# Top-k attention with a gated MLP on one core: the opening's steps issued in an order from a table

## The chip, the core and the metric

The kernel runs on one core of one Trainium2 chip. Five engines work beside each other, each through its own instructions in their order: TensorE (PE in the profile, PEld for its weight loads), VectorE (DVE), ScalarE (ACT), GpSimd (POOL) and SyncE (SP, which here only issues DMAs). Semaphores hold an instruction back until what it reads is written and what it overwrites is read. The metric is the device time in microseconds of one execution; lower is better.

## The reference

Two blocks behind each other. The first is attention over 8 batches and 8 heads, with 576 rows of 64 a head, in which each row keeps its 32 largest scores. The second is an MLP of width 2048 over the 4608 x 512 outputs, whose gate is h * sigmoid(1.702 h).

```python
scores = scale * np.matmul(q, k.transpose(0, 1, 3, 2))
kth = np.partition(scores, -top_k, axis=-1)[..., -top_k:-top_k + 1]
scores = np.where(scores >= kth, scores, -1000000000.0)
scores = scores - np.max(scores, axis=-1, keepdims=True)
attn = np.exp(scores)
attn = attn / (np.sum(attn, axis=-1, keepdims=True) + 1e-09)
x = np.matmul(attn, v)          # heads side by side: (4608, 512)
h = x @ w_in
return (h * (1.0 / (1.0 + np.exp(-1.702 * h)))) @ w_out
```

## The kernel before

**Slots.** The attention is cut into 144 slots, 18 a batch. A slot holds 128 query rows of two heads (of a pair `hp`), that is two score rows of 576 on each of 128 partitions; the last 64 rows of the heads are put together in slots of their own. A slot n goes through these steps, which are spread over later slots:

- `scores(n)` (L330, PE): eight matmuls into the one pair of score banks `s_ps`. `copy_scores(n)` (L345, ACT) copies them to `sc`, of which there are four buffers.
- `pair_up(n)` (L354, DVE): larger and smaller of each pair of columns, into `ranked`. It reads the bank for the last time, so `scores(n + 1)` waits for it.
- `topk(n)` (L374, DVE): four rounds of MAX8 (the eight largest, L386) and three of MATCH_REPLACE8 (remove them, L390) for each of the two halves. The first two rounds run over 288 columns ("half width"), the others over 576. `find` (L1063) issues these fourteen operations of a slot; behind the eighth it issues `pair_up` of the next slot, and behind the ninth `invert` of the slot before.
- `bounds(n)` (L399, POOL): threshold and maximum. `mask(n)` and `exps(n)` (L414, L422, ACT): two passes over each half, with the sum `den`.
- `invert(n)` (L433): 1e-9 is added to the two sums and the reciprocal `rden` is taken on DVE. Up to slot PAIRED = 11 the addition runs on DVE (L439), afterwards on POOL (L437).
- Up to slot 9: `divide` (L443, POOL) makes two diagonal matrices `by` from `rden`, and `turn` (L458) transposes and scales the weights by matmuls on PE, with copies to `pt` on ACT. From slot 10 on: `normalize` (L450, POOL), `split` (L486: a copy on ACT that puts high and low halves of the words apart, and a DMA `rows<-sc` to DRAM), and `turn_by_dma` (L494: a transposing DMA `pt<-rows`).
- `values` (L515), `values_at` (L548), `values_of_two` (L566): weights times v on PE, in two column halves j = 0, 1 of the array (weights of 128 x 64 elements); copies to `xT` on ACT.

**The MLP.** When the four head pairs of a block of 128 rows are there, it is taken in four units: `hidden` (L651, PE, x times w_in), `tanh` (ACT, with a copy `h`), `gate` and `combine` (L685, L702, POOL mostly), `project` (L755, PE, times w_out). The first two blocks ("whole") use matmuls with 128 x 128 weights, the later ones 128 x 64 weights, two of them side by side.

**The opening.** In slots 0 to 10 both weight matrices come in by 32 pieces, which `round_piece` (L136) rounds: `size` and `low` on ACT, `shift` on DVE (L158, TENSOR_SCALARs of 128 x 512), `put_sign` (L148), `add` (L151) and `pool_size` on POOL. `stay_warm` (L170) issues matmuls whose results nobody reads.

**What sets the order.** The order is the order of the calls. `opening()` (L907), then `slot(n)` (L949) for n = 0 to 10, `filling()` (L1138) with a list of steps for each of slots 11 to 20, and `steady_pair(n)` (L1175) for two slots at a time from 21 on. Each engine runs its instructions in the order in which they are issued. All DMAs of the part in question are on SP's queue but three. In `filling_slot` (L1099) a `load_v` that falls due is issued behind `find` and before `scores(n + 2)`; this happens in slot 20, for batch 1.

Of the kernel before, what the change touches and what calls it, by code (L numbers as in the profile page):

```python
# [9 lines left out]
ALU = mybir.AluOpType  # L10
ENG = mybir.EngineType
F32 = mybir.dt.float32
# [7 lines left out]
P = 128  # L20
# [9 lines left out]
TO_ZERO = 2.0**-100  # L30


@with_exitstack
def kernel(
    ctx: ExitStack,
# [23 lines left out]

    nc = tc.nc

    B, H, S, D = q.shape
    C = H * D
# [24 lines left out]
    STEADY = PAIRED + 2  # L90
# [5 lines left out]
    const = ctx.enter_context(tc.tile_pool(name="const", bufs=1))  # L96
# [19 lines left out]
    both_banks = [ps_p.tile([P, 512], F32, name=f"po{i}") for i in range(2)]  # L116

    ident = const.tile([P, P], F32, name="ident")
    make_identity(nc, ident[:])
    win = const.tile([P, CC, DFF], F32, name="win")  # L120
    wout = const.tile([P, FC, C], F32, name="wout")

# [47 lines left out]
    def stay_warm(count, of=ident[:]):  # L170

        none = both_banks[1][:]
        for i in range(count):
            nc.tensor.matmul(none[:, 0:P], lhsT=of, rhs=of, start=True, stop=True)

    def load(name, b, hp, queue=None):

        src = q if name == "q" else k
        if (b, hp) not in loaded:
            home, tag = (ptp, "pt") if b == 0 and hp % 2 else (prp, "pr") if b == 0 and hp else (loads, "qk_l")  # L180
            if b == 1 and hp % 2:
                parts = raws[:, 3, :].bitcast(F32), diagonals[:, 0, :]
                main, ends = [x.rearrange("p (t j d) -> p t j d", j=2, d=D) for x in parts]
                loaded[b, hp] = [main[:, 0:NF, :, :], ends, main[:, NF:, :, :]]
            else:
                t = home.tile([P, 2 * NF + 1, 2, D], F32, name="qk_l", tag=tag)
                loaded[b, hp] = [t[:, 0:NF, :, :], t[:, NF : NF + 1, :, :], t[:, NF + 1 :, :, :], t]
        t = loaded[b, hp]
        heads_of = (lambda j: of_load(name, t)[:, :, j, :]) if queue is None else (lambda j: heads_apart(name, t)[:, j, :, :])
        queue = queue or nc.sync  # L190
        if b > 0 or hp > 1:
            both = src[b, 2 * hp : 2 * hp + 2, 0:FULL, :].rearrange("j (p t) d -> p t j d", t=NF)
            queue.dma_start(of_load(name, t), both)
        else:
            for j in range(2):
                queue.dma_start(heads_of(j), src[b, 2 * hp + j, 0:FULL, :].rearrange("(p t) d -> p t d", t=NF))

        on = slice(0, TAIL) if name == "q" else slice(TAIL, P)
        queue.dma_start(t[1][on, 0, :, :], src[b, 2 * hp : 2 * hp + 2, FULL:S, :].rearrange("h p d -> p h d"))
# [44 lines left out]
    def prepare_ends(b, hp):  # L244
        ends = ps_t.tile([P, 512], F32, name="tp")[:, 0:P]
        turn_qk_ends(b, hp, ends)
        copy_qk_ends(b, hp, ends)
# [45 lines left out]
    def write_all():  # L293
        while writes:
            writes.pop(0)()
# [26 lines left out]
    N = len(slots)  # L322
    PER = N // B
    st = [{} for _ in slots]
# [108 lines left out]
    def invert(n):  # L433

        some = small.tile([P, 2], F32, name="some", tag="sums")
        if n > PAIRED:
            nc.gpsimd.tensor_scalar(some[:], st[n]["den"][:], 1e-9, None, op0=ALU.add)  # L437
        else:
            nc.vector.tensor_scalar_add(some[:], st[n]["den"][:], 1e-9)  # L439
        rden = st[n]["rden"] = small.tile([P, 2], F32, name="rden", tag="inverse")  # L440
        nc.vector.reciprocal(rden[:], some[:])  # L441

# [190 lines left out]
    class Block:  # L633
        def __init__(self, place, rows):
            self.place, self.rows = place, rows
            self.whole = len(blocks_seen) < WHOLE
            self.bank = 1 - len(blocks_seen) % 2
            blocks_seen.append(self)
            self.left = list(range(FC))
            if not self.whole:  # L640
                self.left = [h * (FC // 2) + 2 * u + c for u in range(4) for h in range(2) for c in range(2)]
            self.done = 0
# [202 lines left out]
    for n in by_slot:  # L845
        first = sum(map(len, list(by_slot.values())[:n]))
# [60 lines left out]
    def opening():  # L907

        stay_warm(8, v_tail[:, 0, :, :].rearrange("p j d -> p (j d)"))
        load("q", 0, 0, nc.sync)  # L910
        load("k", 0, 0, nc.scalar)
        for hp in range(2):
            for name in "qk":
                if hp:
                    load(name, 0, hp)
        for x in by_slot[0]:
            load_piece(x)
        prepare_first()
        scores(0)
        pair_first()  # L920
        stay_warm(2)
        for name in "qk":
            prepare_main(name, 0, 1)
        stay_warm(8)
        prepare_ends(0, 1)
        early.extend(round_piece(x) for x in by_slot[0])
        for piece in early:
            piece["size"]()
        scores(1)
        copy_scores(1)  # L930
        prepare_rest()
        for hp in range(2, NP):
            for name in "qk":
                load(name, 0, hp)
        load_v(0, 0)
        for x in by_slot[1]:
            load_piece(x)
# [161 lines left out]
    def filling_slot(n, beside, pool_ahead, behind, pool_behind, late=[]):  # L1099

        todo = later.pop(n, [])
        due = [(fn, args) for fn, args in todo if fn is prepare_by_dma]
        exponentials(n - 1)
        for fn in beside:
            fn()
        for fn in pool_ahead:
            fn()
        find(n, 8)
        for fn, args in todo:
            if fn is load_v:  # L1110
                fn(*args)
        scores(n + 2)
        if n == PAIRED:
            normalize(n - 1)
            split(n - 1)
            copy_scores(n + 2)
        else:
            copy_scores(n + 2)
            normalize(n - 1)
            split(n - 1)  # L1120
        write_all()
        for fn, args in todo:
            if fn not in (prepare_by_dma, load_v):
                fn(*args)
        turn_by_dma(n - 1)
        while turns:
            turns.pop(0)()
        for fn in pool_behind:
            fn()
        bounds(n)  # L1130
        for fn in behind + late:
            fn()
        for fn, args in due:
            fn(*args)
# [40 lines left out]
    def steady_pair(n):  # L1175

        begin, prepare_some = dues(n)
        if live(n - 1):
            exponentials(n - 1)
        combine()  # L1180
        merge_some(3)
        if n > STEADY + 8:
            project_one()
        if n == STEADY + 8:
            brought.pop(0)()
            leave_all()
# [24 lines left out]
        merge_some(3)  # L1211
        if live(n):
            mask(n)
            exps(n)
        tanh(True)
        tanh(True)
        prepare_some()
        project_one()
        find(n + 1, 8)
        if live(n + 3):  # L1220
            scores(n + 3)
        held = [m for m in (n - 3, n - 2) if live(m)]
        o = [ps_t.tile([P, 512], F32, name="o", tag="tp")[:, 0:P] for _ in held]
        values_of_two(held, o)
        if live(n):
            normalize(n)
            split(n)
        write_all()
        while turns:
            turns.pop(0)()  # L1230
        begin(1)
        if live(n):
            turn_by_dma(n)
        gate()
        if live(n + 3):
            copy_scores(n + 3)
        x_of_two(held, o)
        if live(n + 1):
            bounds(n + 1)

    def last_units():
# [7 lines left out]
        project_one()  # L1249
        leave_all()  # L1250

    with tc.manual_schedule():
        opening()
        for n in range(SETTLED + 1):
            slot(n)
        filling()
        for n in range(STEADY + 8, N + 2, 2):
            steady_pair(n)
        combine()
        while ready or to_gate or gated or to_combine or to_project:  # L1260
            last_units()
        merge_some(len(merging), nc.vector)
        write_all()
# [30 lines left out]
```

## Time and profile before

| | us |
|---|---|
| median of 3 runs | 1379.32 (1377.34 to 1382.84) |
| the profiled execution | 1379.59 |
| its span, first to last instruction | 1377.8 |
| PE busy | 1341.2 (97%) |
| DVE busy | 1286.0 (93%) |
| ACT busy | 1164.1 (84%) |
| POOL busy | 964.4 (70%) |
| mean granted clock of TensorE | 0.992 |

The profile is of one execution. Groups of instructions are given by line of the kernel, engine, operation and tiles, as `out<-in`, with their count. A matmul of 32-bit numbers leaves two records. The end of a matmul is modelled and reaches beyond the start of the next one, so durations on PE are read from start to start. Starts are counted from the span's beginning.

### The profile page before, as it was taken

What the parts mean: (1) busy time and instruction counts of PE and PEld (TensorE: products, weight loads), DVE (VectorE), ACT (ScalarE), POOL (GpSimd) and SP (SyncE); (2) the same over time, 40 slices, a digit from 0 to 9 for tenths busy, and PEclk for the clock granted to TensorE, in tenths of its full rate; (3) what the DMA queues carried; (4) which work ended last, traced back from release to release, by engine and by line L of the source; (5) the groups of instructions that cost most, each with busy time, mean ns of one, the idle gap of its engine ahead of it and who ended that gap; (6) DMA issues with size and microseconds to landing.
All of it is one profiled execution on the core that took longest, in us unless ns stands there. A gap on an engine that the chain in (4) does not pass through costs nothing.

```text
span 1377.8 us, 54398 instructions
## 1 busy us (share of the span) xinstructions
PE 1341.2 (97%) x22560; PEld 1205.0 (87%) x22560; DVE 1286.0 (93%) x3392; ACT 1164.1 (84%) x1930; POOL 964.4 (70%) x1758
## 2 busy tenths in 40 slices
PE   7789999999999999999999999999999999999998
PEld 5676578899999999999999999999998999999998
DVE  7999998999999999999999999999999999999912
ACT  6988887998889888988898988888888998888841
POOL 3776676777777776777777777677777777777770
PEclk8999999999999999999999999999999999999999
DMA  7551568787889786977898668988888768855640
GB/s 232 155 163 62 151 159 198 179 196 196 205 210 211 178 189 173 232 193 192 192 227 208 182 174 193 210 198 191 197 211 208 195 176 183 184 142 135 151 118 17
DMA packets 527223, 246.92 MB, mean 179 GB/s; under 512 B 458880, under 2 KB 505472, under 8 KB 526976
## 3 DMA queue, kind: packets, MB, share of 16 engines
q1 hardware_dynamic: 526544, 243.16, 71.5%
q8 instruction: 177, 2.90, 0.9%
q14 instruction: 70, 0.57, 0.1%
q10 hardware_dynamic: 432, 0.30, 0.1%
HBM read 46.01 MB, written 103.42 MB: 108 GB/s over the span
## 4 chain that ended last, share of the span: by engine, by line
PE 79%; DMA 3%; ACT 1%; issue 0%; POOL 0%; SPq 0%; DVE 0%; DVEq 0%; ACTq 0%; POOLq 0%
PE ph L662 32%; PE po L776 28%; PE o L586 10%; PE s_ps L339 9%; DMA pt<-rows 2%; DMA rows<-sc 1%; ACT pr L428 0%; ACT sc L418 0%; ACT sc L490 0%; ACT sc L350 0%; ACT halves L268 0%; ACT raws L794 0%; SPq L221 0%; POOL pr L454 0%; ACT h L681 0%
## 5 line engine op out<-in xcount | busy, mean ns | idle before, releaser
L386 DVE MAX8 top<-ranked 128x8 f32<-128x288 f32 (+1 forms) x1152 | 637.6, 596 | 0.0
L662 PE MATMUL ph<-xT,win 128*64 128x128 f32 (+1 forms) x8544 | 493.8, 273 | 0.0
L662 PEld LDWEIGHTS ph<-xT,win 128*64 128x64 f32 (+1 forms) x8544 | 469.4, 137 | 27.6 <-issue 24.1
L390 DVE MATCH_REPLACE8 ranked<-top,ranked 128x288 f32<-128x288 f32 (+1 forms) x864 | 462.4, 543 | 0.0
L490 ACT COPY sc<-pr 128x2304 uint16<-128x2304 uint16 x134 | 283.4, 2115 | 90.1 <-POOL pr L454 90.0
L454 POOL TENSOR_SCALAR pr<-pr,rden 128x576 f32<-128x576 f32 x268 | 197.9, 748 | 49.2 <-DVE rden L441 47.7
L428 ACT ACTIVATE pr<-sc,low 128x576 f32<-128x576 f32 x288 | 219.9, 769 | 0.0
L418 ACT ACTIVATE sc<-sc,cut 128x576 f32<-128x576 f32 x288 | 208.6, 779 | 4.7 <-POOL cut L404 4.7
L360 DVE TENSOR_TENSOR ranked<-s_ps,sc 128x576 f32<-128x576 f32 x286 | 201.8, 747 | 3.8 <-ACT sc L350 3.8
L776 PE MATMUL po<-raws,h 128*64 128x128 f32 x2112 | 205.3, 273 | 0.0
L776 PE MATMUL po<-wout,h 128*64 128x128 f32 x2112 | 205.3, 273 | 0.0
L350 ACT COPY sc<-s_ps 128x576 f32<-128x576 f32 x286 | 168.5, 642 | 26.9 <-PE s_ps L339 14.4
L437 POOL TENSOR_SCALAR some<-den 128x2 f32<-128x2 f32 x132 | 29.3, 222 | 221.6 <-ACT pr L428 221.4
L339 PE MATMUL s_ps<-qk_t 64*64 64x288 f32 x2304 | 177.6, 421 | 5.6 <-DVE ranked L360 4.4
L691 POOL TENSOR_TENSOR th<-th,h 128x512 f32<-128x512 f32 x134 | 171.8, 1282 | 11.2
L776 PE MATMUL po<-wout,th 128*64 128x128 f32 x2176 | 165.3, 273 | 0.0
L776 PEld LDWEIGHTS po<-raws,h 128*64 128x64 f32 x2112 | 133.8, 137 | 0.0
L776 PEld LDWEIGHTS po<-wout,h 128*64 128x64 f32 x2112 | 133.7, 137 | 0.0
L776 PEld LDWEIGHTS po<-wout,th 128*64 128x64 f32 x2176 | 127.8, 137 | 0.9 <-POOL wout L739 0.4
L339 PEld LDWEIGHTS s_ps<-qk_t 64*64 64x64 f32 x2304 | 76.2, 134 | 58.1 <-issue 14.8
L586 PE MATMUL o<-pt,v_l 128*64 128x128 f32 (+1 forms) x2240 | 124.8, 265 | 0.0
L586 PEld LDWEIGHTS o<-pt,v_l 128*64 128x64 f32 x2240 | 110.3, 137 | 10.1 <-issue 9.5
(118 smaller groups left out, 1647.5 us busy)
## 6 DMA issues: line engine op xcount, KB each, us to landing
rows<-sc SPq DMA_DIRECT2D x134, 576.0 KB, 4.0
qk_rows<-halves SPq DMA_DIRECT2D x24, 576.0 KB, 5.5
out_dram<-raws SPq DMA_DIRECT2D x68, 128.0 KB, 3.7
raws<-in_moe_w_in_dram SPq DMA_DIRECT2D x16, 512.0 KB, 5.1
raws<-in_moe_w_out_dram SPq DMA_DIRECT2D x16, 512.0 KB, 3.7
qk_l<-in_q_dram SPq DMA_DIRECT2D x28, 256.0 KB, 4.4
qk_l<-in_k_dram SPq DMA_DIRECT2D x28, 256.0 KB, 4.2
v_l<-in_v_dram SPq DMA_DIRECT2D x4, 1024.0 KB, 8.8
```

The lines of the kernel that those rows point to most:

```text
L339: nc.tensor.matmul(ps[rows, i, c, 0:HALF], lhsT=qT[b, hps[p]][on, cols], rhs=kT[b, hps[p]][on, FIRST[i] + c * HALF : FIRST[i] + (c + 1) * ...
L360: nc.vector.tensor_tensor(out=ranked[n][:, :, c, :], in0=a, in1=b, op=op)
L386: nc.vector.max(top[:, i, 8 * r : 8 * r + 8], of(r, i))
L390: nc.vector.match_replace(to, top[:, i, 8 * r : 8 * r + 8], of(r, i), LOWEST)
L418: nc.scalar.activation(sc[:, i, :], sc[:, i, :], AF.Prelu, bias=cut[:, i : i + 1], scale=SCALE, alpha=HUGE)
L428: nc.scalar.activation(pr[:, i * S : (i + 1) * S], sc[:, i, :], AF.Exp, bias=low[:, i : i + 1], accum_out=den[:, i : i + 1],)
L454: nc.gpsimd.tensor_scalar(pr[:, i, :], pr[:, i, :], st[n]["rden"][:, i : i + 1], 1.0, op0=ALU.mult, op1=ALU.mult)
L490: nc.scalar.copy(out=halves, in_=pr[:].bitcast(U16).rearrange("p (k h) -> p h k", h=2))
L586: nc.tensor.matmul(o[s][j * D : (j + 1) * D, cols], lhsT=lhsT, rhs=rhs, start=(s, j) not in halves[:k], stop=(s, j) not in halves[k + 1 :],)
L662: nc.tensor.matmul(ph[rows, i * P : (i + 1) * P], lhsT=win[:, c, f * P + rows.start : f * P + rows.stop], rhs=xs[:, x.place, c, :], start= ...
L691: nc.gpsimd.tensor_tensor(out=th[:], in0=th[:], in1=h, op=ALU.mult)
L776: nc.tensor.matmul(both_banks[bank][y * TAIL : (y + 1) * TAIL, to * P : (to + 1) * P], lhsT=a[:, i, :], rhs=weight(w, fs[i])[:, y, :], sta ...
```

## The change

Engine calls go through two small classes. While `nc.collected` is a list, a call is put into it and not issued. `opening`, the eleven `slot`s, `filling` and the `steady_pair`s of 21 and 23 are run so, and then `issue_in_order` issues the collected calls in the order of the table `ORDER` (a part "1600+2" stands for 1600 and 1601). Buffers are still handed out in the order of the code. From `steady_pair(25)` on everything is issued as before.

Besides, the addition of 1e-9 on DVE becomes a TENSOR_TENSOR with a tile `little` that is filled once, and `load_v` in `filling_slot` is no longer issued ahead of the scores but with the other due steps behind `split` and `write_all`.

```diff
+COLLECTED = 25
+
+ORDER = """
+8 11 0+8 9 12 10 13+2 38+4 15+2 24 22+2 25 17 33 26+5 18 31 34 32 19 35 42 36 43+3 20 37 46+4 21 97 50 56+4 98
...
+1526 1589 1476 1665 1510+2 1732+2 1481 1647 1662 1590+8 1527 1538 1555 1443 1528 1512+2 1667 1598+2 1734+2 1557
...
+1567 1477 1649 1568 1740+2 1575 1702+2 1559 1600+2 1641 1602+2 1571 1742+2 1569 1666 1744+2 1604+2 1669 1577
+1606+2 1572 1311 1670 1746+2 1608+6 1675 1533 1614+2 1748+2 1576 1534 1704+2 1671 1616+2 1750+2 1643 1618+2
+1771 1573 1620+2 1677 1622+2 1578 1642 1624+2 1444 1626+2 1636+4 1773 1644 1668 1770 1752+2 1656 1650 1754+2
+1653 1679 1628+2 1706+2 1645 1630+2 1672 1680+3 1654 1683 1772 1684 1673 1685+2 1659 1655 1674 1574 1687 1676
...
+"""
+
+
+class Engine:
...
+    def __getattr__(self, name):
+        do = getattr(self.engine, name)
+
+        def step(*args, **kwargs):
+            if self.engines.collected is None:
+                do(*args, **kwargs)
+            else:
+                self.engines.collected.append(lambda: do(*args, **kwargs))
+
+        return step
...
-    nc = tc.nc
+    nc = Engines(tc.nc)
...
+    little = const.tile([P, 2], F32, name="little")
+    nc.gpsimd.memset(little[:], 1e-9)
...
-            nc.vector.tensor_scalar_add(some[:], st[n]["den"][:], 1e-9)
+            nc.vector.tensor_tensor(out=some[:], in0=st[n]["den"][:], in1=little[:], op=ALU.add)
...
         find(n, 8)
-        for fn, args in todo:
-            if fn is load_v:
-                fn(*args)
         scores(n + 2)
...
         write_all()
         for fn, args in todo:
-            if fn not in (prepare_by_dma, load_v):
+            if fn is not prepare_by_dma:
                 fn(*args)
...
+    def issue_in_order():
+
+        steps, nc.collected = nc.collected, None
...
+        for i in order:
+            steps[i]()
+
     with tc.manual_schedule():
+        nc.collected = []
         opening()
         for n in range(SETTLED + 1):
             slot(n)
         filling()
-        for n in range(STEADY + 8, N + 2, 2):
+        for n in range(STEADY + 8, COLLECTED, 2):
+            steady_pair(n)
+        issue_in_order()
+        for n in range(COLLECTED, N + 2, 2):
             steady_pair(n)
```

In the part of the table that is shown, 1559 is the last MAX8 of slot 16 and 1674 its reciprocal. Of the numbers between them those on DVE are 1666, 1669, 1668 (find of slot 17, half width), 1675, 1677, 1679, 1672 (the same, full width), 1670, 1671 (pair_up of slot 18), and 1770 to 1773 (the first four operations of slot 18); before, 1662 to 1672 stood there.

More of the change, by code (lines that the diff above doesn't have):

```diff
@@ L30, with __init__ @@
 TO_ZERO = 2.0**-100
+COLLECTED = 25
+ORDER = """
[83 rows of a table added]
+"""
+class Engine:
+    def __init__(self, engines, engine):
+        self.engines, self.engine = engines, engine
+    def __getattr__(self, name):
[6 more added lines that the diff above has]
+        return step
+class Engines:
+    def __init__(self, nc):
+        self.collected = None
+        for name in ("tensor", "vector", "scalar", "gpsimd", "sync"):
+            setattr(self, name, Engine(self, getattr(nc, name)))
 @with_exitstack
@@ L118 @@
     ident = const.tile([P, P], F32, name="ident")
-    make_identity(nc, ident[:])
+    make_identity(tc.nc, ident[:])
+    little = const.tile([P, 2], F32, name="little")
+    nc.gpsimd.memset(little[:], 1e-9)
     win = const.tile([P, CC, DFF], F32, name="win")
@@ L1250, in last_units @@
         leave_all()
+    def issue_in_order():
+        steps, nc.collected = nc.collected, None
+        order = list(range(len(steps)))
+        if ORDER.split():
+            order = []
+            for part in ORDER.split():
+                first, _, count = part.partition("+")
+                order += range(int(first), int(first) + int(count or 1))
+        assert sorted(order) == list(range(len(steps)))
+        for i in order:
+            steps[i]()
     with tc.manual_schedule():
+        nc.collected = []
         opening()
```

77 rows, old and new, of the table ORDER are left out of this document.

## The prediction

> **What bounds the kernel now.** I read the page first, then the busy time by stage, then who waited for whom in the stretch that the change touches.
>
> ```profile
> span 1377.8 us, 54398 instructions
> PE 79%; DMA 3%; ACT 1%; issue 0%; POOL 0%; SPq 0%; DVE 0%; DVEq 0%; ACTq 0%; POOLq 0%
> ```
>
> The chain that ended last is PE's. The stages (columns: length, then busy time of PE, PEld, DVE, ACT, POOL, then PE's clock, DMA share, GB/s):
>
> ```profile
> 0.00:10.00 10.00, 8.96 (x77) 7.88 (x78) 1.91 (x7) 2.51 (x3) 1.12 (x9) 1.00 0.62 155
> 10.00:60.00 50.00, 36.37 (x292) 27.27 (x292) 48.99 (x126) 42.99 (x88) 31.34 (x39) 0.83 0.66 209
> 60.00:120.00 60.00, 52.98 (x518) 43.69 (x518) 58.06 (x147) 51.84 (x100) 42.25 (x51) 0.97 0.49 151
> 120.00:210.00 90.00, 84.42 (x880) 60.65 (x880) 85.45 (x230) 77.83 (x140) 65.09 (x92) 1.00 0.52 124
> 210.00:262.00 52.00, 49.89 (x944) 45.34 (x946) 47.92 (x125) 41.39 (x65) 35.88 (x66) 1.00 0.77 195
> 262.00:1200.00 938.00, 936.75 (x16772) 857.85 (x16768) 924.04 (x2446) 836.68 (x1351) 682.10 (x1304) 1.00 0.82 196
> 0.00:262.00 262.00, 232.62 (x2704) 184.82 (x2706) 242.34 (x631) 216.56 (x393) 175.69 (x256) 0.96 0.59 162
> ```
>
> The change collects the steps up to slot 24. In this execution the last of them on PE are the values of steady_pair(23):
>
> ```profile
> 261.15 1.97 PE L586 MATMUL o<-pt,v_l 128*64 128x128 f32 x32
> ```
>
> They end at 263.1. From 262 to 1200 PE idles 938 - 936.75 = 1.25 us. All that follows the collected steps is therefore a block of fixed length behind PE, and what PE gains before 263 us arrives at the end. DVE has 14 us of slack there, so it doesn't become the bound later. Before 262, PE idles 29.4 us and DVE 19.7, of which 8.1 in the first 10 us. DVE is the fuller one: it runs the searches, and PE's scores wait for the bank that it frees.
>
> What DVE and PE wait for (DVE from 10 us on, then PE from 10 us on; total us, times, longest):
>
> ```profile
> DVE some L439 <- ACT pr L428: 4.2, 8, 1.1
> DVE rden L441 <- POOL some L437: 3.7, 4, 1.2
> DVE ranked L360 <- ACT sc L350: 3.2, 2, 3.0
> ...
> PE tp L468 <- POOL by L448: 7.0, 4, 3.5
> PE tp L471 <- ACT pt L476: 6.0, 5, 3.2
> PE tp L237 <- ACT qk_t L234: 5.3, 2, 4.3
> PE s_ps L339 <- DVE ranked L360: 4.4, 5, 1.4
> ...
> PE o L586 <- ACT h L681: 1.4, 2, 0.8
> ```
>
> **The table: what it moves.** I numbered the steps in the order in which the code reaches them: 2,597, the last in steady_pair(23), which is just what the table holds. Against before, 430 of 480 steps stand at another place on DVE, 306 of 351 on ACT, 223 of 249 on POOL, 1,339 of 1,392 on PE, and on SP 4 of 125. Work is neither added nor removed by it, so each engine's floor is its busy time.
>
> *DVE's waits.* Two half-width operations and what followed them, and the groups of full width:
>
> ```profile
> 54.04 0.44 DVE L390 MATCH_REPLACE8 ranked<-top,ranked 128x288 f32<-128x288 f32 x1
> ...
> 54.47 0.44 DVE L390 MATCH_REPLACE8 ranked<-top,ranked 128x288 f32<-128x288 f32 x1
> 55.34 1.29 DVE L439 TENSOR_SCALAR some<-den 128x2 f32<-128x2 f32 x1 [0.43 <-ACT pr L428]
> L386 DVE MAX8 top<-ranked 128x8 f32<-128x576 f32 x100 | 72.4, 746 | 0.0
> L360 DVE TENSOR_TENSOR ranked<-s_ps,sc 128x576 f32<-128x576 f32 x50 | 35.3, 747 | 3.2 <-ACT sc L350 3.2
> ```
>
> invert(n) stands behind nine operations of find(n+1). Between slot 16's last MAX8 and its reciprocal (steps 1559 and 1674) there were eight half-width operations, two pair_ups and one MAX8 of full width; in the table seven of half width, two pair_ups and four of full width, among them slot 18's first four operations. By these rows (0.36 to 0.43 from start to start for half width, 72.4 / 100 or 35.3 / 50, about 0.7, for the others) this is 8 x 0.39 + 3 x 0.7 = 5.2 against 7 x 0.39 + 6 x 0.7 = 6.9 us. Counted so, from start to start, over slots 0 to 23, the mean is 4.4 before and 6.1 in the table.
>
> But ACT's side is stretched too: other steps are put between mask(n) and exps(n), and from mask's start to the end of exps the mean of ACT's own work grows from 2.7 to 3.5 us. Net 1.7 - 0.8 = 0.9 us a slot, against twelve waits for invert of 7.9 us, 0.66 each. Bounds 0 and 7.9; I take three quarters, 6, since the mean wait is less than what was put in front of it and the longest, 1.2, is more.
>
> *PE's cost.* The table mixes hidden, project and values one by one. I counted the changes of the weights' tile (128*128, 128*64, 64*64) between neighbouring steps: 83 before, 176 in the table, nearly all of the 93 more in slots 4 to 17, where hidden and project still use 128*128 and values 128*64. What one costs is seen where the same group has different neighbours:
>
> ```profile
> 61.35 1.09 PE L526 MATMUL o<-pt,v_l 128*64 128x128 f32 x16
> 62.28 0.39 PE L526 MATMUL o<-pt,v_e 128*64 128x128 f32 x4
> 62.49 1.04 PE L526 MATMUL o<-pt,v_l 128*64 128x128 f32 x16
> ...
> 73.87 1.09 PE L526 MATMUL o<-pt,v_l 128*64 128x128 f32 x16
> ...
> 75.11 3.84 PE L662 MATMUL po<-xT,win 128*128 128x128 f32 x32
> ```
>
> The same twenty matmuls take 62.49 - 61.35 = 1.14 us ahead of another 128*64 group and 75.11 - 73.87 = 1.24 ahead of a 128*128 one: 0.10 a change, 93 x 0.10 = 9.3 us. Besides, a 128*64 matmul alone: twenty in two halves take 1.14, 0.057 each, where the 32 of 128*128 take about 0.112 each (3.84 less its 0.27 tail). So two halves run beside each other, and one left without its partner costs between 0 and 0.055 a record more. By counting the unpaired ones in the table this is 0 to 7.3 us; I take 7.3, the row nearer to it.
>
> PE's floor is then 232.6 + 9.3 + 7.3 and 1.0 before its first matmul: 250.2 us. PE has to wait for something on top. In 210 to 262, already full, it idles 2.1 of 52 us, and 1.4 of these are behind h's copy on ACT, which the late rows of the next part push back, so 0.7 of 52; over 250 us that is 3.4. PE ends its collected steps at 253.6 instead of 263.1: **9.5 us earlier**.
>
> **v behind rows.** In slot 20 load_v's three DMAs go from before scores(22) to behind split(19)'s rows. First SP's queue, with the microseconds that each issue took, then who waited, then from issue to landing for rows(19), for v, and for rows as a median:
>
> ```profile
> 223.72 2.82 SPq L282 DMA_TRANSPOSE qk_t<-qk_rows  x1
> 226.58 0.59 SPq L210 DMA_DIRECT2D v_l<-in_v_dram  x1
> 227.22 1.49 SPq L221 DMA_DIRECT2D v_e<-in_v_dram  x2
> 228.76 1.14 SPq L492 DMA_DIRECT2D rows<-sc  x1
> ...
> 237.00 1.18 ACT L350 COPY sc<-s_ps 128x576 f32<-128x576 f32 x2 [4.63 <-DMA rows<-sc]
> ...
> 238.22 1.42 DVE L360 TENSOR_TENSOR ranked<-s_ps,sc 128x576 f32<-128x576 f32 x2 [2.99 <-ACT sc L350]
> ...
> 228.76 8.15 DMA rows<-sc
> ...
> DMA to landing us min/median/max: 6.8/6.8/6.8
> ...
> rows<-sc SPq DMA_DIRECT2D x134, 576.0 KB, 4.0
> ```
>
> rows(19) goes out at 226.6 instead of 228.8, and not behind v's megabyte (8.15 us to landing, the median is 4.0). With the median it lands by 231 instead of 236.9; copy_scores(23) loses its 4.6 us of wait and DVE 3.0. Behind v on SP stands turn_by_dma(19), which waits for rows anyway. v goes out 1.1 us later and is first needed by values of slots 18 and 19 at 243; it had landed 6.8 us after 226.6, so some 8 us of cover stay.
>
> **1e-9 as a tile.** A TENSOR_TENSOR takes the place of twelve TENSOR_SCALARs on DVE.
>
> ```profile
> L439 DVE TENSOR_SCALAR some<-den 128x2 f32<-128x2 f32 x12 | 7.0, 582 | 4.2 <-ACT pr L428 4.2
> L441 DVE RECIPROCAL rden<-some 128x2 f32<-128x2 f32 x24 | 3.8, 160 | 4.1 <-POOL some L437 3.7
> 55.27 1.34 POOL L148 TENSOR_SCALAR raws<-raws 128x512 f16<-128x512 f32 x1
> ```
>
> At 55.34 the addition of two numbers takes 1.29 us, and ends at 56.63 when POOL's put_sign ends at 56.61: it waits out POOL's instruction. A small operation alone is 0.15 to 0.17. The trace has no addition of two SBUF tiles beside a busy POOL: if it is free, 7.0 - 12 x 0.15 = 5.2 us go; if it waits likewise, what counts is where it stands, and in the table 5 of the 12 have a POOL instruction unfinished by the sum of durations before them (2.9 us of rest), so 7.0 - 1.8 - 2.9 = 2.3 go. I take 2.3, the row being that of the operation it replaces. SBUF — State Buffer of the Trainium skill, Who interferes with whom, speaks against this edit: a VectorE instruction with two SBUF inputs contends with a GpSimd one that reads SBUF. No run here shows it yet; by it the 2.3 stands, without it 5.2.
>
> **The sum.** DVE: 262.0 - 6 - 3.0 - 2.3 = 250.7 us, 11.3 earlier. PE: 9.5 earlier. The later one decides: 9.5. This execution took 1379.59 us (1377.8 and 1.8 around it), 0.27 above the median. 1379.6 - 9.5 - 0.3 = **1370 us**.
>
> **Rivals.** *Better than that*: if halves need no partner, PE ends at 246.3 and DVE decides; with all 11.1 us of its waits and 5.2 of the additions gone, 16.3: **1363**. For it, every wait was given more room; against it, ACT's stretch. Chance 0.1.
>
> *The waits only change their place* (no change): DVE's waits come from ACT, which has 216.6 us of work in 262 and runs in order; if its longer stretch from mask to exps eats the room, only the 2.3 and load_v's 3.0 stay, and PE's extra 16.6, which the 29.4 idle cover, take back some: **1376 to 1382**. Against it: 0.9 us net a slot. Chance 0.21. If the additions are blocked everywhere, it costs 2.3 of the forecast: 1372.
>
> *Slower*: PE's tile changes become the path. PE runs in order, and a score that stands behind unpaired halves starts late; DVE then waits for it instead of for ACT. From scores(9) on (94 us before) PE's counted work is 8.8 us more than before. If its idle time there (5.6 in 120 to 210, 2.1 after it) stays, and nothing is gained ahead of it, the end moves by 8.8: **1388**. It decides when PE reaches scores(13) later than DVE has freed the bank; by the sums of work these are level there (about 129 us each). For it: the table's mixing; against it: 20.6 us of PE idle in 10 to 120. Chance 0.17.
>
> **How the numbers follow.** Forecast 0.52, with its own range 1366 to 1374 (PE's waits twice 3.4, or DVE's 11.3). A measurement can tell about 0.5% (6.9 us, here 1372.4 and 1386.2) from no change. Faster: 0.1 + nine tenths of 0.52, and 0.03 of the third case, 0.6; slower 0.17; within 0.23. Range 1363 to 1384, which leaves the slower case out.
>
> **What would show it.** DVE's waits L439 and L441 together fall from 7.9 to about 2; pair_up has no wait of 3 us; PE's idle before 250 falls from 29 to 14 or less while its busy time there rises by 10 to 17; additions take 0.15 to 1.3 us as POOL runs; and the first search of slot 25 starts near 251. The forecast is wrong if PE's busy time in the collected part doesn't rise, or if its end there stays at 260 or later.

## The result, and the profile after

The changed kernel takes **1388.4 us**, the median of six runs (1386.9 to 1394.5), against 1377.5 for the kernel before in the same comparison (six runs, 1374.7 to 1382.8). The ratio is 1.0084 with an interval of 1.0065 to 1.0103: slower by 11 us, where 9.5 us less were forecast. The profiled execution took 1388.0 us, with a span of 1386.2.

The page of after, its span, the busy time of the engines and the chain that ended last. All steps that the table issues carry one line, L133, and those issued directly behind them L131:

```profile
span 1386.2 us, 54405 instructions
...
PE 1358.3 (98%) x22560; PEld 1208.6 (87%) x22560; DVE 1277.7 (92%) x3392; ACT 1164.2 (84%) x1930; POOL 963.2 (69%) x1759
...
PE 89%; ACT 3%; DVE 2%; DMA 2%; issue 1%; POOL 0%; DVEq 0%; ACTq 0%; SPq 0%
PE ph L131 31%; PE po L131 27%; PE o L131 9%; PE s_ps L131 9%; PE po L133 6%; PE o L133 2%; PE tp L133 2%; PE s_ps L133 2%; PE ph L133 1%; DMA pt<-rows 1%; DMA rows<-sc 1%; ACT sc L133 1%; DVE ranked L133 1%; ACT sc L131 1%; DVE top L131 1%
```

The chain now runs through PE's collected steps (po, o, tp, s_ps and ph of L133, 13% of the span together). The work is the same, as many PE records, and yet PE is busy for 1358.3 us where it was 1341.2: 17.1 more. Its idle time, the span less the busy time, fell from 36.6 to 27.9, 8.7 less. The span's 8.4 us are the difference of these two. Where each of them lies is in the stages of after, with the columns as before:

```profile
0.00:10.00 10.00, 8.54 (x62) 7.33 (x62) 0.94 (x5) 1.87 (x2) 1.15 (x10) 1.00 0.67 152
10.00:60.00 50.00, 35.36 (x284) 25.63 (x281) 44.99 (x125) 39.75 (x81) 30.85 (x36) 0.90 0.69 211
60.00:120.00 60.00, 59.05 (x462) 41.59 (x461) 47.49 (x123) 46.00 (x90) 34.98 (x44) 1.00 0.40 124
120.00:210.00 90.00, 89.36 (x840) 61.61 (x837) 83.86 (x229) 76.99 (x140) 65.03 (x86) 1.00 0.47 122
210.00:262.00 52.00, 50.41 (x954) 46.05 (x950) 50.13 (x132) 46.21 (x74) 37.30 (x69) 1.00 0.84 193
262.00:1200.00 938.00, 935.37 (x16718) 856.26 (x16716) 921.79 (x2443) 834.94 (x1348) 679.91 (x1302) 1.00 0.81 196
0.00:262.00 262.00, 242.71 (x2582) 182.22 (x2584) 227.42 (x611) 210.82 (x384) 169.32 (x244) 0.98 0.58 155
```

From 60 to 210 us PE is busy for 148.4 of 150 us, and does it with fewer records than before (1,302 against 1,398): the same matmuls take longer. DVE, which was busy for 58.1 of the 60 us from 60 to 120, is at 47.5. The bound has gone from DVE to PE. Before 60 us PE idles 16.1 us (14.7 before); from 60 to 262 it idles 3.2 (14.7 before).

The last collected work on PE, in its timeline, is a projection of eight records; it ends at 269.9 where the collected part ended at 263.1 before:

```profile
267.53 1.97 PE L133 MATMUL o<-pt,v_l 128*64 128x128 f32 x32
269.33 0.61 PE L133 MATMUL po<-wout,h 128*64 128x128 f32 x8
269.77 0.61 PE L131 MATMUL po<-wout,th 128*64 128x128 f32 x8
```

So 6.8 us of the loss stand at the end of the collected part. The account closes: 17.1 more work, 11.5 less idle time from 60 to 262 and 1.4 more ahead of it make 7.0; the rest of the 8.4 is idle time behind 262.

These busy times are not all at one speed. The clock column has 0.83 and 0.97 in the stages from 10 to 120 us before, and 0.90 and 1.00 in after: there are stretches in which the granted clock is 0.50, and a group takes nearly twice as long in them. In the kernel before, sixteen records of values that take 62.28 - 61.35 = 0.93 us in the rows of the prediction have taken 51.47 - 49.71 = 1.76 one slot earlier, in such a stretch (its row of the stage view first):

```profile
49.70:52.04 2.34, 2.34 (x24) 2.00 (x20) 2.34 (x5) 1.61 (x2) 0.62 (x2) 0.50 0.81 249
49.71 1.97 PE L526 MATMUL o<-pt,v_l 128*64 128x128 f32 x16
51.47 0.64 PE L526 MATMUL o<-pt,v_e 128*64 128x128 f32 x4
```

In the collected part these stretches are 18.2 to 21.7, 25.1 to 31.9, 45.5 to 52.4 and 103.6 to 107.0 us before, and 31.2 to 38.0 and 51.6 to 55.1 us in after; PE is busy for 18.1 and for 7.2 us in them. By these rows 0.47 of that time is lost to the clock, so after is 10.9 x 0.47 = 5.1 us better off (an estimate), and at one clock the table's added work is some 22 us rather than 17.1. What decides where these stretches lie was not tested.

What the added work is can be read in PE's timeline, where the table alternates hidden units, turns and values one matmul at a time (a matmul of whole width leaves two records here):

```profile
81.14 0.43 PE L133 MATMUL tp<-by,pr 128*64 128x128 f32 x2
81.50 0.49 PE L133 MATMUL po<-xT,win 128*128 128x128 f32 x2
81.92 0.43 PE L133 MATMUL o<-pt,v_l 128*64 128x128 f32 x2
82.28 0.49 PE L133 MATMUL po<-xT,win 128*128 128x128 f32 x2
82.70 0.43 PE L133 MATMUL o<-pt,v_l 128*64 128x128 f32 x2
83.06 0.49 PE L133 MATMUL po<-xT,win 128*128 128x128 f32 x2
```

One whole matmul of hidden and one half of values take 82.28 - 81.50 = 0.78 us. In streams of one shape, by the rows of the prediction, they take two records of 0.112 and two of 0.057, 0.34. The 0.44 more are two changes of shape and a half without a partner.

DVE's waits from 10 to 270 us in after (total, times, longest):

```profile
DVE th L133 <- ACT th L133: 10.6, 6, 3.1
DVE ranked L133 <- ACT sc L133: 5.6, 4, 2.6
DVE win L133 <- POOL win L133: 4.2, 1, 4.2
DVE some L133 <- ACT pr L133: 3.4, 5, 1.3
DVE rden L133 <- POOL some L133: 1.8, 1, 1.8
```

The waits that the table was counted on to remove, some and rden, fell from 7.9 to 5.2. A new one of 10.6 stands above them: gate waits for a tanh, and tanh for a hidden unit (ACT's own wait for it grows from 7.7 to 8.9 us).

### The profile page after: what moved, and what is told of

It reads as the page before. It is cut to its first block, busy times and chain, and to the rows that moved or that the text cites. A ratio compares the mean times of both kernels' runs of the same rounds, so it can differ in the third digit from the quotient of the medians.

```text
span 1386.2 us, 54405 instructions
## 1 busy us (share of the span) xinstructions
PE 1358.3 (98%) x22560; PEld 1208.6 (87%) x22560; DVE 1277.7 (92%) x3392; ACT 1164.2 (84%) x1930; POOL 963.2 (69%) x1759
## 4 chain that ended last, share of the span: by engine, by line
PE 89%; ACT 3%; DVE 2%; DMA 2%; issue 1%; POOL 0%; DVEq 0%; ACTq 0%; SPq 0%
PE ph L131 31%; PE po L131 27%; PE o L131 9%; PE s_ps L131 9%; PE po L133 6%; PE o L133 2%; PE tp L133 2%; PE s_ps L133 2%; PE ph L133 1%; DMA pt<-rows 1%; DMA rows<-sc 1%; ACT sc L133 1%; DVE ranked L133 1%; ACT sc L131 1%; DVE top L131 1%
## 5 line engine op out<-in xcount | busy, mean ns | idle before, releaser
L131 DVE MAX8 top<-ranked 128x8 f32<-128x288 f32 (+1 forms) x952 | 526.4, 595 | 0.0
L131 PE MATMUL ph<-xT,win 128*64 128x128 f32 x8064 | 464.3, 273 | 0.0
L131 PEld LDWEIGHTS ph<-xT,win 128*64 128x64 f32 x8064 | 441.2, 137 | 25.9 <-issue 22.8
L131 DVE MATCH_REPLACE8 ranked<-top,ranked 128x288 f32<-128x288 f32 x714 | 381.8, 542 | 0.0
L131 ACT COPY sc<-pr 128x2304 uint16<-128x2304 uint16 x120 | 253.8, 2115 | 88.5 <-POOL pr L131 88.5
L131 POOL TENSOR_SCALAR pr<-pr,rden 128x576 f32<-128x576 f32 x240 | 176.7, 747 | 42.5 <-DVE rden L131 42.5
L131 PE MATMUL po<-wout,h 128*64 128x128 f32 x2000 | 194.3, 273 | 0.0
L131 PE MATMUL po<-raws,h 128*64 128x128 f32 x2000 | 194.3, 273 | 0.0
L131 ACT ACTIVATE pr<-sc,low 128x576 f32<-128x576 f32 x240 | 183.4, 771 | 0.5 <-DMA qk_rows<-halves 0.5
L131 ACT ACTIVATE sc<-sc,cut 128x576 f32<-128x576 f32 x240 | 174.3, 782 | 0.1
L131 DVE TENSOR_TENSOR ranked<-s_ps,sc 128x576 f32<-128x576 f32 x236 | 166.6, 747 | 1.7 <-ACT sc L131 1.7
L131 POOL TENSOR_SCALAR some<-den 128x2 f32<-128x2 f32 x120 | 26.5, 220 | 203.5 <-ACT pr L131 203.5
L131 POOL TENSOR_TENSOR th<-th,h 128x512 f32<-128x512 f32 x123 | 157.3, 1279 | 10.3
L131 PE MATMUL po<-wout,th 128*64 128x128 f32 x2064 | 156.6, 273 | 0.0
L131 ACT COPY sc<-s_ps 128x576 f32<-128x576 f32 x234 | 137.9, 642 | 15.9 <-PE s_ps L131 9.4
L131 PE MATMUL s_ps<-qk_t 64*64 64x288 f32 x1872 | 140.5, 415 | 0.6 <-DVE ranked L131 0.6
L131 PEld LDWEIGHTS po<-raws,h 128*64 128x64 f32 x2000 | 126.4, 137 | 0.0
L131 PEld LDWEIGHTS po<-wout,h 128*64 128x64 f32 x2000 | 126.4, 137 | 0.0
L131 PEld LDWEIGHTS po<-wout,th 128*64 128x64 f32 x2064 | 121.2, 137 | 0.0
L131 PE MATMUL o<-pt,v_l 128*64 128x128 f32 (+1 forms) x2144 | 120.8, 267 | 0.0
L131 PEld LDWEIGHTS o<-pt,v_l 128*64 128x64 f32 x2144 | 106.6, 137 | 9.8 <-issue 9.4
L131 POOL TENSOR_TENSOR h<-th 128x128 f32<-128x128 f32 x248 | 113.7, 458 | 0.3
```

The source lines that it names most:

```text
L131: do(*args, **kwargs)
```

## Experiments

Two theories. **A**: PE pays for the order; changes of the weights' tile make its work longer in slots 4 to 17, where it has no idle time to take that from. **B**: the opening loses; the table lets queues wait for pieces of the weights ahead of the first slots' work. The kernel before had 1376.9 to 1377.3 us beside these runs. Step 411 is the first of slot 4.

**Without the table.** The other two edits alone: `ORDER = ""`.

> The table is empty: the collected steps are issued in the order of the code. What stays is the addition of 1e-9 as a tile and v behind rows. Theory A (PE's tile changes and unpaired halves, counted at 16.6 us, are the whole loss) and theory B (the loss comes from the opening, where ACT waits for weight pieces ahead of the scores' copies) both put the loss into the table: at or below the time before, 1370 to 1377 us. Theory C (one of the two small edits costs the time): 1383 or more. In the profile the additions take about 0.16 us if POOL doesn't hold them, 0.5 if it does, and copy_scores(23) doesn't wait 4.6 us for rows.

Measured: 1376.66 us, ratio 0.9996 (0.9983 to 1.0009). The loss is the table's. From 10 to 270 us DVE's waits are, in this kernel:

```profile
DVE rden L49 <- POOL some L49: 4.9, 4, 2.3
DVE some L49 <- ACT pr L49: 4.6, 8, 1.3
...
DVE ranked L49 <- ACT sc L49: 0.2, 1, 0.2
```

pair_up's 3.0 us of wait behind v's loads are gone, as forecast, and nothing of it shows in the time. The stage from 210 to 262 us of the same kernel has PE busy for 50.4 of 52 us, so an earlier DVE has nothing to hand it:

```profile
210.00:262.00 52.00, 50.40 (x958) 46.07 (x960) 49.71 (x133) 43.58 (x70) 37.44 (x70) 1.00 0.81 195
```

**PE's calls in one piece.** The table, but all matmuls of one call into one tile stand together, at the place of the last of them:

```
+        order = whole(order, nc.calls)
...
+def whole(order, calls):
+    last = {calls[i]: i for i in order if calls[i]}
...
+        elif last[calls[i]] == i:
+            out += [j for j in range(len(calls)) if calls[j] == calls[i]]
```

> The table stays on DVE, ACT, POOL and SP; on PE the matmuls of one call into one tile stand together, where the last of them stood. Tile changes on PE fall from 176 to about 92, unpaired halves to none. Theory A: PE's busy time in the collected part falls by about 16 us, to 234, and the time by 9 to 16, to 1372 to 1379 us. Theory B: scores(3) is still some 7 us late and DVE carries this to the end: 1383 to 1388, though PE's busy time falls as well.

Measured: 1391.23 us, ratio 1.0093 (1.0069 to 1.0118); above the ranges of both theories. PE's work fell, as theory A says, from 1358.3 to 1346.6 us over the span, but its idle time rose from 27.9 to 43.9. PE's waits from 10 to 262 us in this kernel:

```profile
PE s_ps L148 <- DVE ranked L148: 12.5, 5, 7.6
PE tp L148 <- POOL by L148: 5.6, 5, 2.4
PE tp L148 <- ACT xT L148: 3.5, 2, 3.0
```

The longest of them, 7.6 us, is not new (7.5 in after); the others are spread over many steps. That a whole group at its last member's place holds up what stands behind it is a reading that these rows don't prove. The edit changed two things, so it doesn't decide between A and B.

**Each part of the table alone.** First steps 0 to 410 in the code's order and the rest by the table, then the other way round:

```
+        order = list(range(411)) + [i for i in order if i >= 411]
+        order = [i for i in order if i < 411] + list(range(411, len(steps)))
```

> Steps 0 to 410 (the opening and slots 0 to 3) in the order of the code, the others in the table's order. By counting, 161 tile changes and 5.7 of the 7.3 us of unpaired halves stay, so 13 of the 16.6 us. Theory A: PE is still busy without a gap from 60 us on, 1383 to 1388 us. Theory B: ACT's waits for weight pieces and the late scores(3) are gone, 1374 to 1380.

> The reverse: steps 0 to 410 in the table's order, the others in the order of the code. By counting, 96 tile changes, and 2.6 us of the 16.6 stay. Theory A: 1374 to 1380 us. Theory B: ACT waits 6 us for weight pieces before 30 us, scores(3) is late by 6 to 8, and what DVE has lost isn't made good: 1382 to 1388.

Measured: 1389.50 us, 1.0079 (1.0056 to 1.0102), and 1382.70, 1.0036 (1.0026 to 1.0046). The first is 1.5 us above theory A's range, the second is in theory B's: neither theory has the whole of it. The table behind the opening makes the whole loss by itself, and in two stages of code_then_table PE is as full as in after, 147.9 of 150 us:

```profile
60.00:120.00 60.00, 58.37 (x463) 40.74 (x464) 50.05 (x133) 45.19 (x87) 34.52 (x45) 1.00 0.40 127
120.00:210.00 90.00, 89.56 (x856) 62.08 (x852) 84.49 (x228) 77.75 (x137) 67.00 (x90) 1.00 0.49 126
```

The opening's order alone costs 5.7. They don't add up. One reading is that DVE's lateness from the opening is hidden once PE is the bound; another part is the clock, for PE is busy for 16.0 us at the clock of 0.50 in code_then_table and for 7.2 in after. ACT's timeline in table_then_code shows what the opening's order does:

```profile
23.33 0.68 ACT L133 ACTIVATE win<-raws 128x512 f32<-128x512 f32 x1 [3.36 <-DMA raws<-in_moe_w_in_dram]
27.37 1.22 ACT L133 ACTIVATE raws<-raws 128x512 int32<-128x512 uint32 x2 [3.36 <-DMA raws<-in_moe_w_in_dram]
...
30.78 1.47 ACT L133 ACTIVATE sc<-sc,cut 128x576 f32<-128x576 f32 x2
```

ACT waits twice for pieces of w_in, and slot 0's mask behind them starts at 30.8 instead of 20.4 us.

**Halves.** A test of A that leaves the table's order and its numbering as they are: in the collected part each whole matmul of hidden, project and turn becomes two of 64 weight columns inside its step, so that it has the shape of the values.

```
+    def halves(self, out, lhsT, rhs, **kwargs):
...
+        def step():
+            for y in rows:
+                self.engine.matmul(out[y, :], lhsT=lhsT[:, y], rhs=rhs, **kwargs)
...
-                nc.tensor.matmul(tp[:, c * P : (c + 1) * P], lhsT=pr[:, at : at + P], rhs=by)
+                nc.tensor.halves(tp[:, c * P : (c + 1) * P], lhsT=pr[:, at : at + P], rhs=by)
```

> Kernel after, except that in the collected part each 128x128 matmul of a row block's hidden units, of its projection and of a slot's main turn is issued as two 128x64 halves inside one step, so that these no longer differ in shape from the values and the table's numbering stays. Same table. Counted in the table: tile changes 176 -> 98 (83 in the code's order), and a single values half no longer stands between two matmuls of another shape. Theory 'PE pays for the order' (the loss is tile changes and unpaired halves after 60 us, where PE has no idle time to give): PE's busy time in 60 to 210 falls from 148.4 us to 134 to 142 us, and the time from 1388.4 to 1375 to 1382 us; not further, since the opening stays as late as it is. Rival 'the opening' (scores late by waits for pieces of weights): 1386 to 1390 us. Rival 'shapes cost nothing, something else stretches PE': PE's busy time in 60 to 210 stays above 146 us and the time at 1388 us.

> The same edit (128x128 matmuls of the collected part as two 128x64 halves) without the table, steps in the code's order: a control. Tile changes 83 -> 73, so 1 us of PE at most: every theory expects 1374 to 1378 us. If it is faster than that, the halves help by themselves, and after_halves is to be held against it.

> Steps 0 to 410 (opening and slots 0 to 3) in the code's order, the rest by the table, with 128x128 matmuls of the collected part as two halves. Tile changes 161 -> 88. Theory 'PE pays for the order': 1389.5 - 73 x 0.10 - up to 5.7 for unpaired halves = 1376.5 to 1382 us; if the table's removal of waits on DVE is worth anything, this is the kernel that shows it, 1372 to 1376 us. Rival 'the opening': no different from code_then_table, 1389 us.

Measured: 1377.23 us, ratio 1.0000 (0.9990 to 1.0010); 1374.63, 0.9982 (0.9969 to 0.9994); 1375.80, 0.9989 (0.9976 to 1.0002). With the same table, the change of shape alone takes the time from 1388.4 back to 1377.2. Held against the same shapes in the code's order, the table still costs 2.6 us (1377.2 against 1374.6), where it cost 11.7 with whole matmuls (1388.4 against no_table's 1376.7). PE's busy time from 60 to 210 us is 144.9 us, above the 134 to 142 that theory A expected, and below the 146 of the theory that shapes cost nothing. The page of after_halves, the engines:

```profile
PE 1343.3 (98%) x23040; PEld 1202.4 (87%) x23040; DVE 1278.0 (93%) x3392; ACT 1164.6 (85%) x1930; POOL 965.8 (70%) x1759
```

15.0 us of PE's work are gone. In its timeline the same mixture as above now runs at 0.05 us a record:

```profile
81.16 0.27 PE L144 MATMUL po<-xT,win 128*64 128x128 f32 x1
81.22 0.27 PE L133 MATMUL tp<-by,pr 128*64 128x128 f32 x1
81.27 0.27 PE L133 MATMUL o<-pt,v_l 128*64 128x128 f32 x1
81.33 0.27 PE L144 MATMUL po<-xT,win 128*64 128x128 f32 x1
81.38 0.27 PE L133 MATMUL o<-pt,v_l 128*64 128x128 f32 x1
```

Without the table the halves leave 1338.1 of PE's work:

```profile
PE 1338.1 (97%) x23040; PEld 1199.9 (87%) x23040; DVE 1282.7 (93%) x3392; ACT 1164.6 (85%) x1930; POOL 962.7 (70%) x1759
```

What the table does to PE is thus 1358.3 - 1342.3 (no_table) = 16.0 us with whole matmuls, and 1343.3 - 1338.1 = 5.2 with halves.

**The price of one change.** No table; in the row blocks behind the second, every other unit of a hidden group uses whole matmuls where all used halves, which is the same work with three or four changes of shape more in each of 136 groups (four were expected; where scores follow a group, the last change was there before).

```
-                parts = 1 if x.whole else 2
+                parts = 1 if x.whole or i % 2 else 2
```

> Code order (no table), and in every row block after the second the odd ones of the four units of a group use one 128x128 matmul where they used two 128x64 halves: the same work, with 4 changes of tile shape in each of the 136 groups, 544 more than before, nearly all in the part where PE is always busy. It prices a tile change by itself. Theory 'PE pays for the order', at 0.10 us for a change: 1377 + 54 = 1425 to 1437 us. Rival 'a change costs nothing': 1377 us.

Measured: 1463.71 us, 1.0625 (1.0609 to 1.0641). That is above what theory A expected. Neighbouring records of different shape number 800 in its trace and 323 in that of the kernel before: 477 more, and not the 544 of the expectation. 86.4 us for 477 changes are **0.18 us each**, not 0.10. A group of hidden, from its start to that of the scores behind it, takes 4.18 us in mixed_tiles (its label names the first shape alone; the x48 are 32 records of halves and 16 of whole matmuls):

```profile
705.38 4.24 PE L47 MATMUL ph<-xT,win 128*64 128x128 f32 x48
709.56 0.47 PE L47 MATMUL s_ps<-qk_t 64*64 64x288 f32 x4
```

and 3.60 us in the kernel before:

```profile
707.61 3.66 PE L662 MATMUL ph<-xT,win 128*64 128x128 f32 x64
711.21 1.19 PE L339 MATMUL s_ps<-qk_t 64*64 64x288 f32 x15
```

That is 0.58 us for the three changes that are new here, 0.19 each.

**What is left.** For the opening, table_then_code with 17 steps on pieces of the weights moved behind slot 0's exponentials; for PE, after_halves and code_then_halves with the remaining transposes as halves and the two halves of a block side by side, and the same transposes without the table:

```
+        late = [164, 185, 215, 186, 183, 214, 187, 195, 261, 277, 213, 259, 165, 256, 193, 291, 260]
+        order = [i for i in order if i not in late]
+        order[order.index(161) + 1 : order.index(161) + 1] = late
...
+        order = paired(order, nc.pairs)
...
+def paired(order, pairs):
...
+    last = {pairs[i]: i for i in order if pairs.get(i)}
...
+        elif last[key] == i:
+            out += sorted(j for j in order if pairs.get(j) == key)
```

> Kernel table_then_code (opening and slots 0 to 3 by the table, the rest in the code's order), with 17 steps on pieces of the weights (four loads on SP, seven size and low steps on ACT, two shifts on DVE, four steps on POOL) moved, in the table's own order among themselves, from between the first and the last of slot 0's masks and exponentials to behind them. In table_then_code those steps wait for transfers of pieces until 23.3 and 27.4 us, and slot 0's cut comes at 28.0 instead of 20.1 us and its first mask at 30.8 instead of 20.4 us. Theory 'the opening loses by queues that wait for pieces': the mask comes back to 20 to 24 us and the time falls from 1382.7 to 1376.5 to 1379.5 us. Rival 'the opening loses by the order of its searches on DVE', which this leaves alone: 1381 to 1384 us.

> Kernel after_halves (whole table), and besides: the 16 transposes of later q and k columns that the table moves are issued as two halves too, and the two halves of one block of values, of a turn's ends or of a hidden unit, where the table sets them apart, stand together at the place of the later one. Tile changes 98 -> some 80, and no half without its partner. Theory 'PE pays for the order': at 0.16 us for a change and for the unpaired halves together 3 to 6 us off after_halves's 1377.2: 1371 to 1375 us. Rival 'what is left is waits, not PE's work' (values at the later place hold up the scores behind them, as in pe_whole): 1376.5 to 1380 us.

> The same as after_pairs, with steps 0 to 410 in the code's order: the table where it takes waits off DVE, with neither its tile changes nor its opening. Theory 'PE pays for the order': 1375.8 - 3 to 5 = 1371 to 1373.5 us, the fastest of all, and faster than no_table_pairs. Rival: 1375 to 1378 us.

> Control: no table, 128x128 matmuls of the collected part and those transposes as two halves. 7 tile changes less than no_table_halves: 1373.5 to 1375 us by either theory. What code_then_pairs gains over this one is what the table is worth by itself.

Measured: 1383.97 us, 1.0050 (1.0035 to 1.0065); 1378.45, 1.0011 (0.9997 to 1.0026); 1376.93, 0.9998 (0.9989 to 1.0008); 1376.65, 0.9994 (0.9984 to 1.0003). None reached what the first theory expected of it; the first three lie where the rivals had them, and the control 1.7 us above its range. In pieces_behind slot 0's mask does come back:

```profile
23.36 1.44 ACT L133 ACTIVATE sc<-sc,cut 128x576 f32<-128x576 f32 x2 [0.80 <-POOL cut L133]
```

but the time doesn't. Cuts of slots 0 and 1 start at 23.1 and 35.4 us, against 20.1 and 30.3 in the kernel before and 28.0 and 37.3 in table_then_code: the wait was moved more than taken away, for ACT now waits 2.73 us for a piece at 31.9, ahead of slot 1's mask. What the opening loses by stays open. In after_pairs PE's work is 1344.4 us, no less than in after_halves: between neighbours of its own shape a half without a partner costs nothing that shows in single executions.

All kernels side by side, from the first lines of their pages (idle is the span less PE's busy time):

| kernel | median us | span | PE busy | PE idle |
|---|---|---|---|---|
| before | 1377.5 | 1377.8 | 1341.2 | 36.6 |
| after | 1388.4 | 1386.2 | 1358.3 | 27.9 |
| no_table | 1376.7 | 1379.5 | 1342.3 | 37.2 |
| pe_whole | 1391.2 | 1390.5 | 1346.6 | 43.9 |
| code_then_table | 1389.5 | 1389.0 | 1359.4 | 29.6 |
| table_then_code | 1382.7 | 1382.4 | 1345.5 | 36.9 |
| after_halves | 1377.2 | 1374.4 | 1343.3 | 31.1 |
| no_table_halves | 1374.6 | 1372.9 | 1338.1 | 34.8 |
| code_then_halves | 1375.8 | 1373.7 | 1342.9 | 30.8 |
| mixed_tiles | 1463.7 | 1462.5 | 1429.5 | 33.0 |
| pieces_behind | 1384.0 | 1380.2 | 1344.7 | 35.5 |
| after_pairs | 1378.5 | 1375.5 | 1344.4 | 31.1 |
| code_then_pairs | 1376.9 | 1374.1 | 1340.8 | 33.3 |
| no_table_pairs | 1376.7 | 1375.7 | 1342.7 | 33.0 |

These are single executions, and the clock is in them: PE is busy at the clock of 0.50 for 14.4 us in no_table_halves and for 20.8 in no_table_pairs, which by the rate above is 3.0 of the 4.6 us between their busy times. Against no_table_halves, the table takes 3.7 us of PE's idle time (34.8 to 31.1; 4.0 in code_then_halves) and adds 5.2 (4.8) to its work, with 25 (15) changes of shape more. Against no_table_pairs, after_pairs has 1.9 us less idle time and 1.7 more work, and code_then_pairs 0.3 more and 1.9 less. So no gain from the table is shown: whatever waits it takes out, the time of no kernel with it is below that of the same shapes without it. no_table_halves is the one kernel whose interval lies below 1, by 0.2%, and no_table_pairs, with a little more of the same, doesn't confirm it.

## Why the prediction was wrong

*The step that failed* is the line "PE's floor is then 232.6 + 9.3 + 7.3 and 1.0 before its first matmul: 250.2 us" with the 3.4 us that PE would wait on top. It put the added work and the idle time of the whole collected part into one sum, as if the one could fill the other wherever it stands. The added work lies in slots 4 to 17, from 60 us on. Of the 29.4 us of idle time, 14.7 lie ahead of 60 us, where PE has nothing it could do yet, and they stay (16.1 in after). From 60 us on there were 14.7 to take, and PE took 11.5 of them. Forecast were 4.4 us of idle time in the collected part; 19.3 were left before 262. That difference, 14.9, is the way from the forecast end of 253.6 to 268.5; it was 269.9. The stage table of before held both numbers, and the sum went by its last row.

*PE's added work* came out right as a sum, 17.1 us where 16.6 were forecast, but that is partly luck: its terms were wrong, and the clock is in none of them. A change costs 0.18 instead of 0.10, since the row that gave 0.10 showed only the first start of the new shape, and the next one is late too: in mixed_tiles's trace a whole record starts 0.20 us behind the last half and the second one 0.21 behind the first, where 0.10 and 0.11 are usual. 93 x 0.18 = 16.7 stand where the sum had 9.3. Of the some 22 us at one clock this leaves about 5.5 for the halves without partners, by what remains, where 7.3 were taken; the 5.1 us that the clock gave back (an estimate, above) bring the sum down to 17.1.

*DVE's waits*, 6 of 7.9 us taken as saved: 5.2 were left of 7.9 in after, and 4.1 (1.3 and 2.8) in after_halves, 2.7 and 3.8 of the 6 (in no_table they are 9.5, so the table itself takes out 4.3). The cuts of slot 24, which end DVE's collected searches, show what it is worth. In after_halves, in no_table_halves and in code_then_halves, the last collected one starts at:

```profile
L133 POOL TENSOR_SCALAR cut<-top x1: 227/227/227, 256.9 to 256.9; 128x4 f32<-128x4 f32 x1
```

```profile
L49 POOL TENSOR_SCALAR cut<-top x1: 228/228/228, 257.1 to 257.1; 128x4 f32<-128x4 f32 x1
```

```profile
L133 POOL TENSOR_SCALAR cut<-top x1: 227/227/227, 256.4 to 256.4; 128x4 f32<-128x4 f32 x1
```

0.2 and 0.7 us are between the table and the code's order, and the same cut starts at 259.3 in no_table_pairs, so that is inside the spread. Whether an order that keeps the table's places on DVE and PE's groups in one piece would do better wasn't tried in a form that leaves the scores where they are.

*The opening* isn't in the prediction at all. It followed the waits for invert from slot to slot, and not ACT's queue ahead of slot 0's mask, where rounding steps now wait for transfers. Alone the opening's order costs 5.7 us. That these waits are the reason isn't shown: pieces_behind brought slot 0's mask back and stayed at 1384.0. Some 2.6 us of it can be the clock, by the rate above, since PE is busy at 0.50 for 23.6 us in table_then_code and for 18.1 before.

*v behind rows*: DVE's wait of 3.0 went to 0.2, as forecast, and the time didn't move; PE, full from 210 us on, decided, as the prediction's own sum says of the later of the two.

*1e-9 as a tile*: 2.3 us were taken and 5.2 thought possible. The twelve additions went from 7.0 us to this in no_table:

```profile
L49 DVE TENSOR_TENSOR some<-den,little 128x2 f32<-128x2 f32 x12 | 5.7, 474 | 4.6 <-ACT pr L49 4.6
```

and to this in after:

```profile
L133 DVE TENSOR_TENSOR some<-den,little 128x2 f32<-128x2 f32 x12 | 2.1, 173 | 3.4 <-ACT pr L133 3.4
```

In all 4.9 went. The operation alone saves 1.3; the other 3.6 come from the table, which puts ten of the twelve additions where POOL is in no instruction; the prediction had counted on seven.

*The rival that held* is the slower one, at 1388 us: PE's tile changes as the path. It was worked out from the idle time of the stages behind the changes, 5.6 and 2.1, instead of from the whole. Its chance was set at 0.17 for the 20.6 us of PE idle time in 10 to 120, of which 13.6 lie ahead of 60 us and could not bear on it. Its number is partly luck: it had 8.8 us of added work and left the 5.6 and 2.1 standing, where 17.1 were added and 0.6 and 1.6 of those two are left. The sign that was named, PE's collected end at 260 us or later, came: 269.9.

## What to carry to other kernels

Added work is hidden only by idle time that lies behind the point where the work can start: set the two side by side stage by stage, and never across the whole stretch. Compare PE's busy times only with the clock beside them. When a list order mixes matmuls of different tile shapes on TensorE, price every change of shape, or give all of them one shape first; here that one edit took the time from 1388.4 back to 1377.2 us. A reorder that is judged by its waits should also be read queue by queue at the start, where transfers have not landed yet.

## What the hardware showed that was not expected

A change of tile shape costs 0.18 us by mixed_tiles, more than the 0.10 that it adds to the first gap between two starts. The Trainium skill, TensorEngine Tiling (Array Packing), Key Properties, says that a change of the tiling mode drains the engine, while tiles of one mode run independently. The traces are in keeping with both halves of it, though they don't show a drain as such: 0.78 us for a pair of matmuls of two shapes, and 0.05 us a record where all have one.

An addition with two inputs in SBUF does wait for POOL. In no_table DVE's

```profile
66.53 1.03 DVE L49 TENSOR_TENSOR some<-den,little 128x2 f32<-128x2 f32 x1 [0.43 <-ACT pr L49]
```

starts just behind POOL's

```profile
66.47 1.35 POOL L49 TENSOR_SCALAR raws<-raws 128x512 f16<-128x512 f32 x1
```

and ends at 67.56, 0.26 us ahead of the recorded end of put_sign. The rule that the prediction took from the Trainium skill, SBUF — State Buffer, Who interferes with whom, agrees with this, and the free addition of the prediction's other bound is not seen: the operation takes 0.14 to 0.18 us only with put_sign over or less than 0.45 us from its recorded end. The TENSOR_SCALAR of the kernel before, with one such input, waited as well (1.29 us at 55.34, in the prediction's rows), so these traces don't show that the second input is the reason.
